# Attention and mixture of experts: the values of a pair of heads in three loads, with the global keys' rows copied on the chip

## The chip, the cores and the metric

One Trainium2 chip, one of its cores. The metric is device time of one execution in microseconds; the median of three runs of the kernel before is 718.49 us (716.6 to 720.79). A core has TensorE (PE, with its weight loads PEld), VectorE (DVE), ScalarE (ACT), GpSimd (POOL), SyncE (SP), which here issues the plain DMAs, and 16 DMA engines.

## The reference

Batch 8, 8 heads, 512 local and 32 global positions, head dimension 64. Per head, a global query attends to all 544 keys; a local query attends to the 32 global keys and to the local keys at most 32 positions away. Then each token of the 8 x 544 = 4352, with the 512 values of its heads side by side, goes to one of 8 experts (a greedy assignment with a capacity of 544 tokens each), and the expert applies two matrices with a ReLU between them.

```
s_g = scale * q_g @ k_all.T ;  out_g = softmax(s_g) @ v_all
s_l = scale * [q_l @ k_g.T , where(|i-j| <= 32, q_l @ k_l.T, -1e9)]
out_l = softmax(s_l) @ [v_g ; v_l]
x = heads side by side;  h = relu(x[mask_e] @ w1[e]);  out[mask_e] = h @ w2[e]
```

All data are float32.

## The kernel before

The attention comes first, then the routing (which token goes to which expert), then the experts. Only the attention's loads are changed.

**Keys and values by blocks.** Local positions are cut in 16 blocks of 32. A local block of queries needs its own block of keys, both neighbours, and the global keys: 4 x 32 = 128 rows, one matmul's width. On the host, `_blocks` puts a copy of the global block after every second local block, so that each such set of 128 rows lies together. For the values the 128 rows of a window lie along the partitions. The even windows are loaded: window w of head h is at `vw[:, 0, h, w]`, 65 columns (64 values and a column of ones, which sums the softmax). In an even window the partitions 0 to 31 hold the block before, 32 to 63 the global keys' rows, 64 to 95 the own block and 96 to 127 the next one. The rows of the global keys are thus the same in all 8 even windows of a head. The odd windows hold the same blocks at other partitions, and GpSimd makes them from the even ones with four copies (L119 to L122).

**Tiles.** A pair of heads (`b`, `p`; 32 pairs) has a tile `qk` (queries and keys, three loads) and a tile `vw` (128 partitions x 2 parities x 2 heads x 8 windows x 65). Seven buffers of each are in rotation. Before the change the even half is loaded in two DMAs, one per head, each 128 partitions x 2080 B; `load_v` is a generator that yields after each.

**Steps.** A step of the attention is a pair of heads with its local queries, or a batch entry's four pairs with their global queries: scores (`S`, on TensorE), mask and exp (DVE, ACT), transposes (`T`), evacuation by ACT, values (`O`: TensorE with weights `pt` and the tile vw, both parities), normalisation (DVE). The order of the steps' parts is written out by hand; all of TensorE's instructions of the attention come through one helper, so they have line L83 and are told apart by tiles.

**The order of loads.** A planner sorts the loads by the step that needs them. Each time that TensorE's issued work has grown by a fixed amount (by the kernel's own estimate) `tick` takes one piece: the next part of a generator. `paced` (L94) issues a DMA on SyncE's queue, which first waits for the last TensorE instruction issued before it. SyncE works through its queue in order. The first loads (L145 to L150) are issued without this order, before the steps begin.

**Stores.** The result of each batch entry goes to a buffer `xd` in DRAM, through the same queue. The experts later gather from it and from the weights with indirect DMAs that GpSimd issues; those run on a queue of their own.

Of the kernel before, what the change touches and what calls it, by code (L numbers as in the profile page):

```python
# [18 lines left out]
B, H, SL, SG, D = 8, 8, 512, 32, 64  # L19
# [44 lines left out]
def attention(ctx, tc, A, consts, xd, ident, L, nbatch, rt=None):  # L64
    nc = tc.nc
# [5 lines left out]
    qk, vw, xs, xg = {}, {}, {}, {}  # L71
# [21 lines left out]
    def paced(dst, src):  # L93
        d = nc.sync.dma_start(dst, src)  # L94
        if pe.last is not None:
            tc.add_manual_dep(d.ins, pe.last.ins.name,
                              mybir.DependencyInfo(mybir.DependencyClass.Sync, mybir.DependencyReason.DATA), reason="pace")
# [11 lines left out]
    def load_v(b, p):  # L109
        t = ld.tile([128, 2, 2, NW // 2, D + 1], F32, name="vw", bufs=7)  # L110
        vw[b, p] = t
        ev, od = t[:, 0], t[:, 1]
        n = NW // 2
        for h in range(2):
            w = n * (D + 1)
            paced(ev[:, h].rearrange("p w d -> p (w d)"), A["vw"][b, p, :, h * w:h * w + w])
            if h == 0:
                yield
        nc.gpsimd.tensor_copy(od[0:64], ev[64:128])  # L119
        nc.gpsimd.tensor_copy(od[64:96], ev[32:64])  # L120
        nc.gpsimd.tensor_copy(od[96:128, :, :n - 1], ev[64:96, :, 1:])
        nc.gpsimd.tensor_copy(od[96:128, :, n - 1:], ev[64:96, :, n - 1:])  # L122
        yield
# [22 lines left out]
    nc.sync.dma_start(mask.rearrange("p a b -> p (a b)"), A["mask"])  # L146
    nc.sync.dma_start(ident, A["ident"])
    now(load_qk(0, 1), load_v(0, 0))
    nc.sync.dma_start(wg.rearrange("p a b -> p (a b)"), A["wg"])
    now(load_qk(0, 2), load_v(0, 1))  # L150
    warm = ac.tile([128, 128], F32, name="warm")
    nc.vector.memset(warm, 0.0)
# [266 lines left out]
    for i, u in enumerate(steps):  # L419
        for q in [u[0].q] if isinstance(u[0], Local) else range(NP):  # L420
            for f, t in ((load_qk, i - LA), (load_v, i + 1)):
                k = f, u[0].b, q
                need[k] = min(t, need.get(k, t))
                left[k] = left.get(k, 0) + 1
# [784 lines left out]
```

## Time and profile before

| | before |
|---|---|
| median of the runs | 718.49 us |
| the profiled execution's own time | 718.45 us |
| its span, first to last instruction | 716.7 us |
| granted TensorE clock, mean | 0.968 |
| busy: PE, PEld, DVE, ACT, POOL | 657.4, 538.4, 477.0, 321.2, 223.0 us |
| read from and written to HBM | 83.49 and 17.83 MB |
| DMA queues, share of 16 engines over the span | q1 (SyncE's) 21.7%, q0 (GpSimd's) 20.4%, q8 (instructions) 0.7% |
| first to last load of values issued | 4.5 to 191.9 us |

A row of a group or a waits view names line, engine and operation, then what is written and read. In a view of waits the numbers are the microseconds in total, the times it happened and the longest. In a timeline they are the start, the duration over a merged row, and in brackets the idle time before it and what ended that; "issue" there is time in which the engine waited for nothing that the profile shows. The DMA share is the mean over the 16 engines.

### The profile page before, as it was taken

The page shows a single profiled execution, that of the slowest core. Times are in us where ns is not written, and L with a number is a line of the kernel's source. Part 1 is how long each engine was busy: PE and PEld are TensorE (multiplying, and loading weights), DVE is VectorE, ACT ScalarE, POOL GpSimd, SP SyncE. Part 2 cuts the span into 40 slices and gives each one's busy share as a digit, 9 for nine tenths or more (in the row PEclk, how much of TensorE's full clock was granted, in tenths as well). Part 3 has the DMA queues.
Part 4 walks back from the last instruction along what each step waited for, and adds up shares of the span by engine and source line. Part 5 has one row for each costly group of instructions (what it writes and reads, how often), then busy time and mean ns, then how long its engine had stood idle before and what let it go on. Part 6 is the DMA issues. An engine that isn't in the chain of part 4 may idle for free.

```text
span 716.7 us, 23878 instructions
## 1 busy us (share of the span) xinstructions
PE 657.4 (92%) x9972; PEld 538.4 (75%) x9972; DVE 477.0 (67%) x1758; ACT 321.2 (45%) x870; POOL 223.0 (31%) x249
## 2 busy tenths in 40 slices
PE   7797989889992599999999999999999999999997
PEld 6576666667771498778779879878978877988985
DVE  3678777787877887767767777767776774640510
ACT  5766767767840144343234244234333342641421
POOL 3565446654510500440240241142043025312002
PEclk9999999999995599999999999999999999999999
DMA  8788879887410530720540351162063065331001
GB/s 305 223 260 255 260 235 287 279 263 247 156 67 2 180 119 1 265 82 16 182 158 22 117 201 45 62 223 78 2 229 132 1 250 177 115 114 53 16 16 48
DMA packets 39580, 102.86 MB, mean 144 GB/s; under 512 B 4912, under 2 KB 14384, under 8 KB 35376
## 3 DMA queue, kind: packets, MB, share of 16 engines
q1 hardware_dynamic: 29232, 49.95, 21.7%
q0 software_dynamic: 10240, 51.39, 20.4%
q8 instruction: 78, 1.28, 0.7%
q14 instruction: 30, 0.25, 0.1%
HBM read 83.49 MB, written 17.83 MB: 141 GB/s over the span
## 4 chain that ended last, share of the span: by engine, by line
PE 76%; DVE 9%; issue 6%; DMA 4%; ACT 3%; POOL 1%; SPq 0%; POOLq 0%; DVEq 0%; ACTq 0%
PE H L1059 22%; PE Y L1087 21%; PE T L83 10%; PE S L83 7%; PE O L83 6%; PE R L617 4%; PE H L931 2%; DVE r_G L546 2%; DVE w2l L546 2%; PE Y L1077 2%; DMA xg<-xd,idx 1%; DMA out_dram<-y,idx 1%; PE Y L1107 1%; DVE r_pm L546 1%; ACT w2h L908 1%
## 5 line engine op out<-in xcount | busy, mean ns | idle before, releaser
L1059 PE MATMUL H<-xh,w1h 128*128 128x272 f32 x512 | 151.5, 296 | 1.9 <-DVE hl L546 1.5
L1059 PE MATMUL H<-xh,w1l 128*128 128x272 f32 x512 | 150.0, 293 | 0.0
L1059 PE MATMUL H<-xl,w1h 128*128 128x272 f32 x512 | 149.9, 293 | 0.0
L1061 ACT ACTIVATE hh<-H 128x272 fp32r<-128x272 f32 x128 | 50.9, 398 | 130.3 <-PE H L1059 125.8
L1087 PE MATMUL Y<-w2h,hh 128*128 128x512 f32 x256 | 103.9, 406 | 0.0
L1087 PE MATMUL Y<-w2l,hh 128*128 128x512 f32 x256 | 102.7, 401 | 0.0
L1087 PE MATMUL Y<-w2h,hl 128*128 128x512 f32 x256 | 102.4, 400 | 0.0
L1059 PEld LDWEIGHTS H<-xh,w1h 128*128 128x128 f32 x512 | 96.5, 188 | 5.3 <-DVE hl L546 2.5
L1059 PEld LDWEIGHTS H<-xl,w1h 128*128 128x128 f32 x512 | 96.5, 188 | 0.6
L1059 PEld LDWEIGHTS H<-xh,w1l 128*128 128x128 f32 x512 | 96.4, 188 | 0.3
L938 POOL DMA_INDIRECT out_dram<-y,idx x40 | 41.4, 1034 | 137.3 <-ACT y L1029 79.1
L173 ACT ACTIVATE p<-p,nm 128x128 f32<-128x128 f32 x256 | 78.0, 396 | 7.9 <-DVE nm L168 7.9
L168 DVE CUSTOM_DVE_ANT_0 p<-S,mask 128x128 f32<-128x128 f32 x256 | 56.7, 286 | 28.5 <-PE S L83 27.8
L546 DVE SCALAR_TENSOR_TENSOR hl<-H,hh 128x272 fp32r<-128x272 f32 x128 | 54.5, 434 | 23.6 <-ACT h L1063 12.8
L546 DVE TENSOR_TENSOR w2l<-w2r,w2h 128x512 fp32r<-128x512 f32 x64 | 43.2, 688 | 37.3 <-ACT w2h L908 36.9
L892 POOL DMA_INDIRECT w1r<-in_w_dram,widx x16 | 15.7, 980 | 163.0 <-DVE r_a L546 122.4
L83 PE MATMUL S<-qk 64*32 64x128 f32 (+2 forms) x2240 | 53.7, 299 | 12.2 <-issue 8.0
L1029 ACT ACTIVATE y<-Y 128x512 f32<-128x512 f32 (+1 forms) x40 | 23.2, 594 | 92.6 <-PE Y L1087 66.5
L119 POOL COPY vw<-vw 64x1040 f32<-64x1040 f32 x32 | 33.5, 1047 | 89.2 <-DMA vw<-in_vw_dram 51.3
L1087 PEld LDWEIGHTS Y<-w2h,hh 128*128 128x128 f32 x256 | 48.2, 188 | 15.7 <-issue 5.9
L908 ACT ACTIVATE w1h<-w1r 128x512 fp32r<-128x512 f32 x64 | 36.4, 622 | 47.1 <-DMA w1r<-in_w_dram,widx 47.1
L1087 PEld LDWEIGHTS Y<-w2h,hl 128*128 128x128 f32 x256 | 48.2, 188 | 10.0 <-issue 0.2
(177 smaller groups left out, 1214.0 us busy)
## 6 DMA issues: line engine op xcount, KB each, us to landing
vw<-in_vw_dram SPq DMA_DIRECT2D x64, 260.0 KB, 4.1
qk<-in_qk_dram SPq DMA_DIRECT2D x64, 216.0 KB, 3.7
qk<-in_qk_dram SPq DMA_DIRECT2D x32, 272.0 KB, 4.3
xd<-xs SPq DMA_DIRECT2D x28, 256.0 KB, 4.1
xd<-xs SPq DMA_DIRECT2D x1, 1024.0 KB
xg<-xd,idx POOLq DMA_INDIRECT x40, 3.6
out_dram<-y,idx POOLq DMA_INDIRECT x40, 2.8
cf<-in_cf_dram SPq DMA_DIRECT2D x1, 512.0 KB
```

Source lines behind the costliest of these rows:

```text
L83: s.last = op(o, w, x, **kw)
L119: nc.gpsimd.tensor_copy(od[0:64], ev[64:128])
L168: nc.vector.tensor_tensor_reduce(s.p[:, c, :], s.st[:, c, :], mask[:, c, :], -SCALE, BIG, ALU.add, ALU.min, s.nm[:, c:c + 1])
L173: nc.scalar.activation(s.p[:, c, :], s.p[:, c, :], AF.Exp, bias=s.nm[:, c:c + 1], scale=-1.0)
L546: return op(*args, **kw)
L617: s.nc.tensor.matmul(out, *args, **kw)
L908: nc.scalar.activation(hi, raw, AF.Copy)
L938: nc.gpsimd.indirect_dma_start(out=out, out_offset=bass.IndirectOffsetOnAxis(ap=rt.idx[ph][:n, t:t + 1], axis=0), in_=y[:n], in_offset=None)
L1029: nc.scalar.activation(y[:n], p[:n], AF.Copy)
L1059: nc.tensor.matmul(p, w[d][:, fs], x[:, d, q], start=(d + k == 0), stop=(d + k == 5))
L1061: nc.scalar.activation(hh[:, f, q], p, AF.Relu)
L1087: nc.tensor.matmul(p, h[:, f, q], w[f], start=(f + k == 0), stop=(f + k == 9))
```

## The change

The even half of a pair's values comes in three DMAs. The first brings, on partitions 32 to 63, window 0 of each head alone: 32 partitions x 2 heads x 260 B = 16,640 B. The second brings partitions 64 to 127 with all windows of both heads, 64 x 4160 B = 266,240 B. After the generator's yield the third brings partitions 0 to 31, 32 x 4160 B = 133,120 B. A new GpSimd copy, ahead of the four that there were, writes windows 1 to 7 of partitions 32 to 63 from window 0: 32 partitions x 2 x 7 x 65 elements. The four old copies, the arrays on the host and everything else stay as they were.

```diff
         n = NW // 2
-        for h in range(2):
-            w = n * (D + 1)
-            paced(ev[:, h].rearrange("p w d -> p (w d)"), A["vw"][b, p, :, h * w:h * w + w])
-            if h == 0:
-                yield
+        src = A["vw"][b, p].rearrange("p (h w d) -> p h w d", h=2, d=D + 1)
+        paced(ev[32:64, :, 0], src[32:64, :, 0])
+        paced(ev[64:128], src[64:128])
+        yield
+        paced(ev[0:32], src[0:32])
+        g = ev[32:64, :, 0:1]
+        nc.gpsimd.tensor_copy(ev[32:64, :, 1:], g.to_broadcast([32, 2, n - 1, D + 1]))
         nc.gpsimd.tensor_copy(od[0:64], ev[64:128])
```

## The prediction

> **What bounds the kernel now.** I read the page first: TensorE is busy nearly throughout, and there are three DMA queues that matter.
>
> ```profile
> PE 657.4 (92%) x9972; PEld 538.4 (75%) x9972; DVE 477.0 (67%) x1758; ACT 321.2 (45%) x870; POOL 223.0 (31%) x249
> q1 hardware_dynamic: 29232, 49.95, 21.7%
> q8 instruction: 78, 1.28, 0.7%
> ```
>
> Queue q1 carries all loads and stores of the attention. Queue q8 moves 1.28 MB in 78 packets, 16 KB each; TensorE has 2 x 9972 = 19,944 instructions, 256 to a packet, so I read q8 as the fetch of TensorE's program.
>
> The change touches only the attention, the first 213 us. The table of busy time by stage cuts it in the part with loads (35 to 185 us) and the tail, in which nearly all loads are done:
>
> ```profile
> 35.00:185.00 150.00, 132.99 (x4208) 101.92 (x4212) 116.22 (x654) 106.76 (x335) 81.94 (x101) 0.98 0.82 259
> 185.00:213.00 28.00, 27.28 (x837) 22.56 (x825) 21.68 (x114) 18.85 (x56) 8.40 (x11) 1.00 0.29 99
> ```
>
> The columns are stretch, length, then busy time of PE, PEld, DVE, ACT and POOL, the granted clock, DMA share and GB/s. With the DMA engines 82% busy TensorE idles 17.0 of 150 us; with them 29% busy it idles 0.7 of 28 us. The table of waits says for what, from 15 to 185 us and, last line, from 185 to 213 us:
>
> ```profile
> PE O L83 <- issue: 9.0, 9, 2.3
> PE S L83 <- issue: 8.0, 7, 2.2
> PE T L83 <- ACT p L173: 1.2, 1, 1.2
> PE S L83 <- DVE nm L168: 1.1, 1, 1.1
> PE T L83 <- issue: 1.0, 1, 1.0
> ...
> PE T L83 <- ACT xt L315: 0.7, 1, 0.7
> ```
>
> So 18.0 us in 17 waits are "issue": nothing in the program held TensorE back. No tile, DMA of data or engine costs it more than 1.2 us. One such wait, in the timeline, and the DMA queues in the stretch that ends with it (33.00 to 35.94 us):
>
> ```profile
> 35.94 0.42 PE L83 MATMUL O<-vw,pt 128*32 128x65 f32 x11 [2.34 <-issue]
> ...
> q1 hardware_dynamic: 502, 0.96, 89.3%
> q8 instruction: 1, 0.02, 2.1%
> ```
>
> TensorE stands still from 33.60 to 35.94 us, one fetch packet moves, and the engines are full of data. My reading: a fetch waits behind the data packets queued on its DMA engine, and TensorE runs dry. The attention is bound by TensorE plus the lateness of its program. A DMA therefore costs time here not by landing late but by standing ahead of a fetch.
>
> **The change, part by part.** First the load on q1 in that stretch (35 to 185 us):
>
> ```profile
> q1 hardware_dynamic: 22309, 38.16, 80.1%
> q8 instruction: 34, 0.56, 1.5%
> ...
> vw<-in_vw_dram SPq DMA_DIRECT2D x51, 260.0 KB, 4.1
> ```
>
> *Bytes.* 38.16 MB in 80.1% of 150 us is 318 GB/s while the engines work. A pair's values are two DMAs of 266,240 B: 532,480 B, 1.67 us of all 16 engines. These are 51 x 266,240 B = 13.6 MB of 38.16, 36% of the queue. After the change a pair has 16,640 B (32 partitions, two rows of 260 B each), 266,240 B on partitions 64 to 127 and 133,120 B on 0 to 31. The two large ones at 318 GB/s are 1.26 us. The small one is 64 packets: by bytes 0.05 us, and as 64 packets of the mean length (80.1% x 16 x 150 us / 22,309 = 86 ns) over 16 engines 0.34 us. I take 0.1, near the bytes, as its rows are a seventh of the mean packet. Sum 1.36 us, which is 0.31 us (19%) less, if the engines keep their rate.
>
> *Rate.* No load of before covers fewer than 128 partitions. The nearest rows are the scatters of the expert outputs, of 32 rows (window 310.80 to 311.40 us) and of 128 rows (318.75 to 319.75 us), each alone on the engines:
>
> ```profile
> DMA packets 32, 0.07 MB, mean 109 GB/s; under 512 B 16, under 2 KB 16, under 8 KB 32
> q0 software_dynamic: 32, 0.07, 46.1%
> ...
> DMA packets 80, 0.26 MB, mean 262 GB/s; under 512 B 16, under 2 KB 16, under 8 KB 80
> q0 software_dynamic: 80, 0.26, 68.9%
> ```
>
> Each has 16 packets of a few bytes that mark its end; the others are 4 KB. On 32 partitions one takes 46.1% x 16 x 0.60 us / 16 = 277 ns, on 128 it takes 68.9% x 16 x 1.00 us / 64 = 172 ns: 1.6 times as long on few partitions. These read SBUF and the loads write it, so the bounds for the loads are 1.0 (no such effect) and 2 (two engines take turns throughout; the 32-row case has one packet per engine, so they overlap in part only). I take 1.6, the one row there is: 1.26 x 1.6 + 0.1 = 2.11 us for a pair, 0.44 us (26%) more than now. With 2 it is 2.62 us, 0.95 us (56%) more.
>
> [...]
>
> *From the queue to TensorE.* How much stands ahead of a fetch? The view of the tile vw gives the time from issue to landing:
>
> ```profile
> L94 SPq DMA_DIRECT2D vw<-in_vw_dram x64: 327/332/1649, 4.5 to 191.9; - x64
> L119 POOL COPY vw<-vw x32: 1043/1046/1057, 10.2 to 195.8; 64x1040 f32<-64x1040 f32 x32
> L120 POOL COPY vw<-vw x32: 1042/1047/1057, 11.3 to 196.9; 32x1040 f32<-32x1040 f32 x32
> L121 POOL COPY vw<-vw x32: 940/941/949, 12.4 to 198.0; 32x910 f32<-32x910 f32 x32
> L122 POOL COPY vw<-vw x32: 291/292/293, 13.3 to 198.9; 32x130 f32<-32x130 f32 x32
> ...
> DMA to landing us min/median/max: 2.6/4.1/5.8
> ```
>
> The median is 1.5 us above the least, so I put the typical queue at 1.5 us; 36% of it is values. At 1.6 a fetch waits 1.5 x 0.36 x 0.26 = 0.14 us longer. There are 34 fetches in the stretch: 4.8 us if each of them passes it on, 2.4 us if only the 17 that are late now do. The other bound is that every added microsecond of the queue meets a fetch: 25.5 pairs x 0.44 = 11 us. I take 4.8, because a queue at 80% that gets 11 us (7% of the stretch) more work also makes fetches late that are in time today.
>
> *The start.* TensorE waits for queries and keys behind the first pair's values:
>
> ```profile
> 4.53 0.91 SPq L94 DMA_DIRECT2D vw<-in_vw_dram  x2
> 11.62 1.29 PE L83 MATMUL S<-qk 64*32 64x128 f32 x64 [1.42 <-DMA qk<-in_qk_dram]
> ```
>
> One pair is ahead of that transfer, so the wait moves by +0.4 us (bounds -0.3 and +0.9). The third issue, 0.46 us here, is hidden while the transfer is behind others on the engines; uncovered it would add that.
>
> *SyncE and GpSimd.* 32 more issues at 332 ns are 10.6 us for SyncE, which in the first 300 us spends more than that waiting for TensorE's pace:
>
> ```profile
> SPq L94 <- PE T L83: 62.2, 87, 5.1
> SPq L94 <- PE O L83: 47.0, 43, 9.5
> ```
>
> The new GpSimd copy writes 32 x 910 elements, as many as L121: 0.94 us a pair, 30 us in all. It waits for the small DMA; queued behind it are the pair's four other copies and, once, the clearing of pg (2.09 us from 17.95 us), which two more such copies move by 1.9 us to an end at 21.9 us, ahead of its first use at 24.19:
>
> ```profile
> 17.95 2.09 POOL L157 MEMSET pg<- 128x768 f32 x3
> 24.19 0.58 ACT L240 ACTIVATE pg<-S,gm 128x384 f32<-128x384 f32 x1
> ```
>
> In exchange the four old copies no longer need the last transfer (partitions 0 to 31 aren't among their sources), and the new one can run while partitions 64 to 127 are still on their way. The tightest place is the last pair:
>
> ```profile
> 191.25 0.95 SPq L94 DMA_DIRECT2D vw<-in_vw_dram  x2
> 195.81 1.05 POOL L119 COPY vw<-vw 64x1040 f32<-64x1040 f32 x1 [5.51 <-PE O L83]
> 198.85 1.60 PE L83 MATMUL O<-vw,pgt 128*32 128x64 f32 x95
> 198.88 0.29 POOL L122 COPY vw<-vw 32x130 f32<-32x130 f32 x1
> ```
>
> TensorE starts on these values as the last copy ends. Uncovered, the new copy costs 0.9 us there, once; started a DMA issue earlier it gains at most 0.3 us. I take 0. DVE and ACT get nothing new.
>
> *Sum.* The profiled execution took 718.45 us (span 716.7 and 1.75 around it; the median of the runs is 718.49, practically the same). 718.45 + 4.8 + 0.4 = 723.65 us. With the bounds of each term (2.4 to 11, and -0.3 to 0.9, last pair -0.3 to 0.9) this case spans 720.5 to 731.
>
> **The rivals.**
>
> *The bytes win.* If the loads to 64 and 32 partitions keep the full rate, the queue ahead of a fetch shrinks by 1.5 x 0.36 x 0.19 = 0.10 us, times 34 is 3.5 us, and 0.3 at the start: 714.65 us. For it: TensorE's idle falls with the DMA share in the stages. Against: the scatter rows. It decides if a packet on few partitions takes less than 1.25 times its usual time (1.25 x 1.26 + 0.1 = 1.67).
>
> *Nothing moves.* The "issue" waits could have a cost of their own, whatever the queue; then neither less nor more load changes them: 718.45 us. The tail without such waits speaks against it, but it also has other steps. [...] The same time results if bytes and rate just cancel.
>
> *Full contention.* If two engines take turns throughout (factor 2), a pair needs 0.95 us more; 25.5 of them are 24 us in 150, and the share goes from 0.82 to 0.98. The queue is then 1.5 x 0.36 x 0.56 = 0.30 us longer at least, times 34 is 10.3, and 0.9 at the start: 729.65 us. It decides where the engines have no idle time left.
>
> *GpSimd late.* If the copies depended on all three DMAs, each pair would be ready 0.9 us later; only the last pair has no margin: 719.35 us.
>
> **How the numbers follow.** Half a per cent, 3.6 us, is about what a measurement tells from no change. Chances: forecast 0.36 and full contention 0.12 (slower, 0.48 together); bytes win 0.24, of which 0.02 ends within 3.6 us (faster 0.22); nothing moves 0.25 and GpSimd late 0.03 (same 0.30). The forecast's own range is 720.5 to 731; to leave out no more than 0.2 it reaches down to 712, past the bytes' case, and to 731, past most of full contention.
>
> **What would show it.** In the stretch of loads: the mean length of q1's packets per byte (now 318 GB/s while busy; about 1.6 times slower on the values alone would bring it near 270), DMA share up from 0.82 in spite of 3.7 MB less, TensorE's "issue" waits up from 18.0 us by about 5, landing of the two large DMAs no earlier. If "issue" falls together with the DMA share, the bytes won; if it stays while the share moves, the fetch isn't the cause. The last pair's first GpSimd copy should begin before 195.8 us. A time above 731 or a wait for vw on TensorE in most steps would make the whole reading wrong.

## The result, and the profile after

| | before | after |
|---|---|---|
| median of 6 runs each | 719.04 us (716.6 to 720.79) | 725.33 us (723.07 to 726.75) |
| after / before, 95% interval | | 1.0094 [1.0067, 1.0122] |
| profiled execution, its span | 718.45, 716.7 us | 725.3, 723.5 us |
| mean granted clock | 0.968 | 0.970 |

The kernel is 0.94% slower. The prediction said 723.6 us with a range of 712 to 731, slower being the likeliest.

From the page of the kernel after, the busy times and the queue q1 that the prediction showed of before:

```profile
PE 657.5 (91%) x9972; PEld 538.2 (74%) x9972; DVE 478.4 (66%) x1758; ACT 320.9 (44%) x870; POOL 252.0 (35%) x281
...
q1 hardware_dynamic: 26672, 46.23, 21.5%
```

TensorE does the same work in the same busy time (657.4 us before, 657.5 after). GpSimd has 29 us more (the copies). Queue q1 moves 3.7 MB less than before, yet its share of the engines hardly falls (21.7% to 21.5%, of a longer span).

The table of busy time by stage, of after:

```profile
35.00:185.00 150.00, 127.64 (x4121) 97.57 (x4110) 113.17 (x629) 104.07 (x330) 104.05 (x123) 0.99 0.79 238
185.00:213.00 28.00, 27.50 (x860) 21.72 (x859) 22.31 (x124) 21.61 (x65) 13.32 (x17) 1.00 0.30 88
```

In the part with loads TensorE now idles 22.4 of 150 us instead of 17.0, with the engines *less* busy than before (0.79, was 0.82). In the tail it idles 0.5 us, before 0.7. The table of waits from 15 to 185 us, of after:

```profile
PE O L83 <- issue: 8.7, 14, 1.2
PE S L83 <- issue: 7.9, 6, 3.0
PE T L83 <- issue: 4.1, 3, 1.8
PE S L83 <- DVE nm L170: 2.2, 2, 1.1
PE S L83 <- DMA qk<-in_qk_dram: 1.7, 1, 1.7
```

"Issue" is 20.7 us in 23 waits, where it was 18.0 in 17, and a wait for queries and keys is new in this stretch. One profile each does not make much of the difference: in the first experiment below, where the time is that of before, "issue" is 15.4 us. The queue behind this, 35 to 185 us, of after:

```profile
q1 hardware_dynamic: 20218, 35.08, 77.6%
q8 instruction: 32, 0.52, 1.6%
...
qk<-in_qk_dram SPq DMA_DIRECT2D x49, 216.0 KB, 4.8
...
vw<-in_vw_dram SPq DMA_DIRECT2D x25, 260.0 KB, 4.2
...
vw<-in_vw_dram SPq DMA_DIRECT2D x25, 130.0 KB, 3.9
vw<-in_vw_dram SPq DMA_DIRECT2D x25, 16.2 KB, 4.2
```

35.08 MB in 77.6% of 150 us is 301 GB/s while the engines work; before it was 318. 25 pairs of values are 10.4 MB. If the other 24.68 MB still go at 318 GB/s (77.6 us), the values take 116.4 - 77.6 = 38.8 us, by this estimate 1.55 us a pair: less than the 1.67 of before, more than the 1.36 that were estimated for their bytes at 318 GB/s. Of the view of the tile vw, a row of before, and then rows of after:

```profile
L83 PE MATMUL O<-vw,pt x2048: 217/219/317, 14.8 to 208.3; 128*32 128x65 f32 x187
```

```profile
L83 PE MATMUL O<-vw,pt x2048: 217/219/317, 16.9 to 214.3; 128*32 128x65 f32 x187
...
L94 SPq DMA_DIRECT2D vw<-in_vw_dram x96: 326/588/1634, 4.5 to 198.6; - x96
...
DMA to landing us min/median/max: 2.4/3.8/5.5
```

In a row of this view stand the number of instructions, the least, median and greatest duration in ns, and the start of the first and of the last in us. TensorE's last matmul on a local step's values starts at 214.3 us instead of 208.3: 6.0 of the 6.8 us by which the span grew lie in the attention. The median issue of a load of values now holds SyncE for 588 ns, not 332. Attention ends of single profiles, which come from several chips, differ by some us (205.8 us in the profile of the first experiment), so the verdicts below rest on ratios and the profiles only show where to look.

### The profile page after: what moved, and what is told of

The parts are those of the page before. It is cut to its first block, busy times and chain, and to the rows that moved or that the text cites. A ratio compares the mean times of both kernels' runs of the same rounds, so it can differ in the third digit from the quotient of the medians.

```text
span 723.5 us, 23984 instructions
## 1 busy us (share of the span) xinstructions
PE 657.5 (91%) x9972; PEld 538.2 (74%) x9972; DVE 478.4 (66%) x1758; ACT 320.9 (44%) x870; POOL 252.0 (35%) x281
## 3 DMA queue, kind: packets, MB, share of 16 engines
q1 hardware_dynamic: 26672, 46.23, 21.5%
## 4 chain that ended last, share of the span: by engine, by line
PE 48%; DVE 3%; DMA 2%; issue 2%; ACT 1%; POOLq 0%; DVEq 0%; ACTq 0%
PE Y L1089 21%; PE H L1061 21%; PE R L619 3%; PE H L933 2%; PE Y L1079 2%; DVE w2l L548 1%; DMA w1r<-in_w_dram,widx 1%; DVE r_G L548 1%; ACT w2h L910 1%; DMA xg<-xd,idx 1%; PE Y L1095 0%; DMA out_dram<-y,idx 0%; DVE r_pm L548 0%; DVE w1l L548 0%; DVE hl L548 0%
## 5 line engine op out<-in xcount | busy, mean ns | idle before, releaser
L940 POOL DMA_INDIRECT out_dram<-y,idx x40 | 39.9, 997 | 135.8 <-ACT y L1031 82.2
L83 PEld LDWEIGHTS S<-qk 64*32 64x32 f32 x2240 | 33.2, 106 | 31.8 <-issue 19.5
```

Source lines behind the costliest of these rows:

```text
L83: s.last = op(o, w, x, **kw)
L940: nc.gpsimd.indirect_dma_start(out=out, out_offset=bass.IndirectOffsetOnAxis(ap=rt.idx[ph][:n, t:t + 1], axis=0), in_=y[:n], in_offset=None)
```

## The experiments

Each ratio is to the kernel before in runs on the same chip, with its 95% interval; the experiments ran on four chips, so two of them are compared by their ratios. A difference of two ratios has half-widths added in squares. The diffs show the lines that stand in place of the loads of before, or that are added to them; `src` is that of the change.

**1. The copy alone.** The kernel before plus the new copy after its loads.

```diff
+        g = ev[32:64, :, 0:1]
+        nc.gpsimd.tensor_copy(ev[32:64, :, 1:], g.to_broadcast([32, 2, n - 1, D + 1]))
         nc.gpsimd.tensor_copy(od[0:64], ev[64:128])
```

> The loads of before (two DMAs of 128 partitions, all bytes) with the new GpSimd copy added, which here writes again what the loads brought. Theory RATE (transfers to few partitions run slower, so the queue ahead of loads and fetches is no shorter): 719 us, no change. Theory ISSUE (the third DMA and its longer issue hold SyncE's queue, so that loads come later): 719 us. Theory COPY (GpSimd's added 0.94 us a pair makes the values late): 724 to 726 us, with waits of TensorE for GpSimd's copies.

Measured: 1.0011 [0.9978, 1.0045]. The copy costs nothing that can be told apart from none; it isn't the cause.

**2. Three DMAs, all bytes, all partitions.**

```diff
+        paced(ev[:, 0, 0], src[:, 0, 0])
+        paced(ev[:, 0, 1:], src[:, 0, 1:])
+        yield
+        paced(ev[:, 1], src[:, 1])
```

> All bytes of before, all on 128 partitions, but in three DMAs a pair (window 0 of head 0; windows 1 to 7 of head 0; head 1), no new copy. RATE: 719 to 720 us, since no transfer has few partitions. ISSUE: 722 to 726 us if an issue takes about 0.6 us as in the changed kernel, about 720.5 if it stays at 0.33 us. COPY: 719.

Measured: 1.0042 [1.0010, 1.0074], 3.0 us. The third issue has a price of its own, or the burst of two DMAs before the yield has.

**3. Both loads on half the partitions**, all bytes, no copy.

```diff
+        paced(ev[64:128], src[64:128])
+        yield
+        paced(ev[0:64], src[0:64])
```

> All bytes of before in two DMAs a pair, each on 64 partitions (64 to 127, then 0 to 63), no new copy. RATE: rows of 4160 B at 250 ns, eight per engine, are 2.0 us a pair where before takes 1.69, some 10 us more of queue time over 32 pairs: 723 to 727 us. ISSUE: two issues as before, 719 us, or 720 to 721 if an issue to few partitions is longer by itself. COPY: 719.

Measured: 1.0234 [1.0187, 1.0282], 16.9 us, the slowest of all and more than twice the expected 4 to 8 us, with the same bytes and the same number of DMAs as before. Queue q1 and then the tile vw, of this kernel:

```profile
q1 hardware_dynamic: 18428, 36.89, 85.9%
```

```profile
L83 PE MATMUL O<-vw,pt x2048: 217/219/317, 18.6 to 219.8; 128*32 128x65 f32 x187
...
L94 SPq DMA_DIRECT2D vw<-in_vw_dram x64: 465/477/1573, 4.5 to 203.5; - x64
...
DMA to landing us min/median/max: 3.3/5.1/8.1
```

The engines are busier for fewer bytes in the stretch (286 GB/s), the loads land 1 us later at the median, and each issue takes 145 ns longer than before.

**4. The change's bytes on all partitions.** Three DMAs of 16,896, 266,240 and 133,120 B, and a GpSimd copy in place of the bytes left out.

```diff
+        paced(ev[:, 1, 4, 0:33], src[:, 1, 4, 0:33])
+        paced(ev[:, 0], src[:, 0])
+        yield
+        paced(ev[:, 1, 0:4], src[:, 1, 0:4])
+        nc.gpsimd.tensor_copy(ev[:, 1, 4:], ev[:, 1, 0:4])
```

> The bytes and the number of DMAs of the changed kernel, but each on 128 partitions: 132 B rows, head 0 with 2080 B rows, windows 0 to 3 of head 1 with 1040 B rows. Windows 4 to 7 of head 1 are not loaded; GpSimd copies windows 0 to 3 there (about 0.3 us a pair), so the values of that head's last windows are not the reference's. RATE: a pair takes about 1.35 us of the engines where before takes 1.69, so the waits for the fetch shrink by 3 to 4 us: 714 to 717 us. ISSUE: three issues, as in the changed kernel: 721 to 725 us, 718 to 719 if issues stay at 0.33 us.

Measured: 0.9990 [0.9962, 1.0019], no gain where fewer bytes alone were expected to bring 2 to 5 us. Against experiment 2, with as many DMAs on as many partitions, the fewer bytes gain 0.52% (± 0.43). Against the change itself (1.0094), with the same bytes and number of DMAs, it is the partitions that cost: 1.04% (± 0.40), or the longer issues that come with them (median 588 ns against 382 here); experiments 8 and 9 separate these two.

**5. Loads with nothing beside them.** Eleven loads into an unread tile ahead of everything else, on various partitions.

```diff
+    sc = ac.tile([128, 1040], F32, name="sc")
+    sv = A["vw"][0, 0]
+    for lo, hi in ((0, 128), (64, 128), (0, 128), (32, 96), (0, 128), (0, 32), (0, 128), (0, 64), (0, 128)):
+        nc.sync.dma_start(sc[lo:hi], sv[lo:hi])
...
```

> The kernel before, with eleven loads of one pair's values put ahead of everything, each alone (it waits for the one before, which writes some of the same rows): 128 partitions between the others, 64 to 127, 32 to 95, 0 to 31, 0 to 63, and last the small one of 260 B rows and 128 partitions again. RATE, with partitions sharing ways in by halves (0 to 63 and 64 to 127): a 4160 B row takes about 165 ns on 128 partitions and on 32 to 95, which has both halves, and 250 to 320 ns on 64 to 127, 0 to 63 and 0 to 31. If few partitions are slow by their number alone, 32 to 95 is as slow as 64 to 127. If neither, all rows take about 165 ns and the slow rows of the changed kernel come from its company. ISSUE: the issues to few partitions take SyncE longer (about 0.6 us) than those to 128 (0.35 to 0.45 us) even with nothing else under way.

The DMA queues of this kernel while partitions 64 to 127 are loaded (4.38 to 7.95 us), then 0 to 127 (7.95 to 11.40), then 32 to 95 (11.40 to 14.27), and later 0 to 31 (17.75 to 20.09):

```profile
q1 hardware_dynamic: 80, 0.27, 28.8%
...
q1 hardware_dynamic: 144, 0.53, 49.2%
...
q1 hardware_dynamic: 80, 0.27, 32.5%
...
q1 hardware_dynamic: 48, 0.13, 19.8%
```

Share x 16 x length over the number of rows (64, 128, 64, 32; the 16 packets under 512 B that come with each load counted as nothing) is 257, 212, 233 and 232 ns for a row of 4160 B. By the same working partitions 0 to 63 take 238 ns, and the four other loads of 128 partitions from 198 to 214. So alone, few partitions cost here 1.1 to 1.25 times per row, much less than the scatter rows' 1.6 and less than expected. These are single loads, and equal ones differ by 8%: that 32 to 95 would be faster than 0 to 63 or 0 to 31, as expected of halves, is not shown here.

**6. One load for all**, 128 partitions x 4160 B.

```diff
+        paced(ev.rearrange("p h w d -> p (h w d)"), A["vw"][b, p])
+        yield
```

> All bytes of before on 128 partitions in one DMA a pair (rows of 4160 B), no new copy. ISSUE: one issue less a pair than before takes off about what the third one added in the kernel with three full DMAs (0.4%): 0.995 to 0.998 of before. RATE: rows on 128 partitions keep their rate, 1.00; if rows of 4160 B were the cause and not the partitions, it is slower, 1.01 or more. A burst twice as long ahead of a fetch could cost some of the gain: up to 1.005.

Measured: 1.0036 [1.0006, 1.0066]. One issue fewer gains nothing when its 532 KB come at once. Whether the burst takes the gain away, or that a pair's loads are now one piece of the pace less, is not shown. Rows of 4160 B are not slow in themselves here: queue q1 in 35 to 185 us has 321 GB/s, before 318.

```profile
q1 hardware_dynamic: 18282, 37.47, 77.7%
```

**7. A slower pace of the loads**, on the kernel before.

```diff
-        if pe.work >= 0.62:
-            pe.work = min(pe.work - 0.62, 1.0) if piece() else 0.62
+        if pe.work >= 0.66:
+            pe.work = min(pe.work - 0.66, 1.0) if piece() else 0.66
```

> The kernel before with each load issued after 0.66 instead of 0.62 us of TensorE's work by the kernel's own estimate, in all three places of that constant. If the queue ahead of the fetch sets TensorE's idle time, loads spread out further leave it shorter: 0.993 to 0.998 of before, with fewer waits for issue than 18 us between 15 and 185 us. If the queue doesn't matter: 1.00. If loads then come too late: above 1.003, with waits for DMA of qk or vw.

Measured: 1.0044 [1.0008, 1.0080], not the gain that was expected of a shorter queue. The "issue" waits are 12.2 us where before has 18.0, a wait of 2.2 us for queries and keys came up, and the kernel was no faster. The waits from 15 to 185 us, of this kernel:

```profile
PE O L83 <- issue: 6.0, 8, 1.5
PE S L83 <- issue: 5.4, 5, 1.9
PE S L83 <- DMA qk<-in_qk_dram: 2.2, 1, 2.2
...
PE T L83 <- issue: 0.8, 1, 0.8
```

**8. The change without its small DMA.** GpSimd fills partitions 32 to 63 from elsewhere.

```diff
+        paced(ev[64:128], src[64:128])
+        yield
+        paced(ev[0:32], src[0:32])
+        g = ev[64:96, :, 0:1]
+        nc.gpsimd.tensor_copy(ev[32:64], g.to_broadcast([32, 2, n, D + 1]))
```

> The changed kernel without its small DMA: the global keys' rows are not loaded, and GpSimd's new copy fills all eight windows of partitions 32 to 63 from window 0 of partitions 64 to 95 (1.05 us a pair), so the values of the global keys are not the reference's. The two large DMAs stay. ISSUE: two issues instead of three, about 0.4% less than the changed kernel: 1.004 to 1.006 of before. RATE alone: the large DMAs decide, 1.008 to 1.010.

**9. The same on the middle partitions.** Two loads of the same bytes on 64 and 32 partitions, but the first on 32 to 95.

```diff
+        paced(ev[32:96], src[32:96])
+        yield
+        paced(ev[0:32], src[0:32])
+        nc.gpsimd.tensor_copy(ev[96:128], ev[64:96])
```

> As the kernel without the small DMA (two DMAs of 64 and 32 partitions, one added GpSimd copy of 1.05 us), but the large DMA brings partitions 32 to 95 instead of 64 to 127, and GpSimd fills 96 to 127 from 64 to 95, so the values of those rows are not the reference's. Same bytes, same number of DMAs and of partitions in each. RATE by halves of the partitions: the large transfer now reaches both halves, its 4160 B rows take about 200 ns as in the kernel with one load, the mean over all values' rows falls from 250 to about 220 ns, and the time is 1.000 to 1.004 of before. If the number of partitions decides, or ISSUE: 1.006 to 1.010, as without the small DMA (1.008).

Measured: 1.0079 [1.0047, 1.0111] for 8 and 1.0012 [0.9985, 1.0039] for 9. The two kernels differ in nothing but which partitions the first load and the copy take, and their ratios by 0.67% (± 0.42). Against the change itself, experiment 8 has the third DMA less and gains 0.15% (± 0.42): here the third issue has no price that can be told from none. Queue q1 from 35 to 185 us, first of 8, then of 9:

```profile
q1 hardware_dynamic: 18323, 35.01, 77.7%
```

```profile
q1 hardware_dynamic: 17944, 34.30, 72.5%
```

300 GB/s against 315. By the working used above (399,360 B a pair, 25 pairs, the rest at 318 GB/s) a pair takes by estimate 1.51 and 1.29 us; its bytes at 318 GB/s are 1.26. On 32 to 95 the penalty is nearly gone, though the issues are no shorter (medians 476 and 522 ns). The traces have each packet's time, so this can be seen without the subtraction: from 35 to 185 us a packet of 4160 B, which only loads of values have, takes on average 210 ns in experiment 6 (128 partitions), 217 in 9, 245 in the change, 247 in 8 and 263 in 3. That partitions share their ways in by halves, as the expectation has it, was the author's assumption: the direction agrees (217 against 247 ns), the cause is not shown.

**10. Half of the bytes.** Only the first head's values are loaded; the second gets a copy of them.

```diff
+        paced(ev[:, 0].rearrange("p w d -> p (w d)"), A["vw"][b, p, :, :w])
+        yield
+        nc.gpsimd.tensor_copy(ev[:, 1], ev[:, 0])
```

> The kernel before with only head 0's values loaded (one DMA of 128 partitions, 2080 B rows); GpSimd copies them to head 1 (about 0.55 us a pair), so head 1's values are not the reference's. 8.5 MB and 32 DMAs less. RATE, that is, the queue ahead of the fetch sets TensorE's idle time: the queue loses about 27 of 155 us, and of 18 us of waits for issue some 6 to 10 go: 0.985 to 0.992 of before. If the bytes on the queue don't matter to TensorE: 1.00. ISSUE alone: 32 issues less, 0.996.

Measured: 0.9948 [0.9913, 0.9982], less than expected of the queue; the 0.996 expected of the 32 issues alone lies in the interval. The queue and, in the second fence, the waits from 15 to 185 us, of this kernel:

```profile
q1 hardware_dynamic: 18650, 31.43, 66.3%
```

```profile
PE O L83 <- issue: 6.5, 9, 1.8
PE S L83 <- issue: 5.8, 9, 1.4
...
PE T L83 <- issue: 0.3, 1, 0.3
```

The waits are 12.6 us, about as few as in experiment 7, where the queue is hardly shorter (78.9%). And 80.1% - 66.3% of 150 us is 20.7 us of queue, for 3.8 us of time (0.52% of 723.07): some 0.2 us per us of queue, and part of that may be the issues'.

**11. An almost empty DMA more for each pair** (64 B), on the kernel before.

```diff
+    tiny = ac.tile([16, 8 * 32], F32, name="tiny")
...
+        k = 4 * b + p
+        paced(tiny[:, 8 * k:8 * k + 1], A["vw"][b, p, :16, :1])
```

> The kernel before with one DMA more a pair that moves almost nothing (16 partitions x 4 B into a tile that nobody reads), issued ahead of the first of the pair. ISSUE: 1.003 to 1.005 of before, if a third issue of 0.35 to 0.6 us on SyncE is what the kernel with three full DMAs pays. If the third issue is hidden by SyncE's waits for TensorE's pace, as the prediction had it: 0.999 to 1.001.

**12. Two of them, but none in the first four pairs**, whose loads stand at the start: 56 DMAs.

```diff
+        for i in range(2 if b else 0):
+            paced(tiny[:, 8 * k + 4 * i:8 * k + 4 * i + 1], A["vw"][b, p, :16, :1])
```

> The kernel before with two of the almost empty DMAs a pair (16 partitions x 4 B into a tile that nobody reads), but only from the second batch entry on: 56 added issues in the paced part and none before or in the first steps, where the kernel with one a pair for all pairs had four. If ISSUE costs in the paced part, where SyncE waits for TensorE's pace: 1.005 to 1.008 of before, with the end of the attention later by 3 to 6 us. If its cost lies at the start, where SyncE issues without a break and TensorE waits for the first queries and keys: 0.999 to 1.002.

Measured: 1.0034 [1.0006, 1.0062] for 11 and 1.0071 [1.0046, 1.0096] for 12: 2.4 us for 32 added issues and 5.1 us for 56, 0.08 and 0.09 us each. So added DMAs cost in the paced part too, not only at the start, and SyncE's waits do not hide them. Of experiment 12, in three views: queue q1 in 35 to 185 us, TensorE's waits for "issue" from 15 to 185 us, and SyncE's waits over the first 300 us:

```profile
q1 hardware_dynamic: 23666, 37.91, 78.3%
```

```profile
PE O L83 <- issue: 12.3, 9, 2.5
PE S L83 <- issue: 7.3, 8, 1.8
PE T L83 <- issue: 3.0, 3, 1.4
```

```profile
SPq L94 <- PE T L83: 46.5, 67, 5.1
SPq L94 <- PE O L83: 36.3, 30, 8.9
...
SPq L94 <- DMA qk<-in_qk_dram: 10.0, 18, 2.5
```

The engines are no busier than before, yet "issue" went from 18.0 to 22.6 us. SyncE waits less for TensorE's pace (82.8 us in these two rows, 109.2 before) and now 10.0 us for landings of qk (0.4 before, 1.7 in experiment 11). The trace's semaphores tell what these waits are: this program's plain DMAs use eight semaphores in turn (100 and 102 to 108, for all 201 DMAs of before and all 233 of after), and each wait is for the DMA issued eight places earlier, which has to land first. Two added DMAs in a row bring that limit nearer, so part of experiment 12's price may be this wait and not the issue; experiment 11 and the change (2.0 us) hardly meet it.

## Why the prediction was right, and which steps failed

**The sum.** Forecast +5.2 us; measured 6.85 us between the profiled executions, and 0.94% of 719.04 us, 6.8 us. The experiments split it so:

| part | forecast | measured |
|---|---|---|
| GpSimd's copy | 0 | +0.1% ± 0.3 (1) |
| SyncE's third issue | 0 | +0.34% ± 0.28 (11) to +0.42% ± 0.32 (2): 2.4 to 3.0 us; +0.15% ± 0.42 (after against 8) |
| fewer bytes | -0.31 us of queue a pair | -0.52% (4 against 2): -3.7 us |
| half the partitions | +0.75 us of queue a pair | +0.67% (8 against 9) to +1.04% (after against 4): 4.8 to 7.5 us |
| start | +0.4 us | not measured alone |
| last pair | 0 | 0 |

With 0.34, 0.67 and the other parts the sum is 0.1 + 0.34 - 0.52 + 0.67 = 0.6%, with the larger figures 1.04%; 0.94% lies between. This is no sharp test: each part is uncertain by 0.3 to 0.4%, and the larger figure for the partitions uses the change's own time. Bytes and partitions together come to +1.1 to +3.8 us, where the forecast had 4.8; the third issue, which it left out, adds up to 2.4 to 3.0 us. (The bounds of the forecast's terms add up to 720.25 and 731.25, not 720.5 and 731.)

**Loads to few partitions run slower per byte: right, mis-sized.** The factor was taken as 1.6 from the scatter rows; it is about 1.2 (245 to 263 against 210 ns a packet, 1.51 against 1.26 us a pair). So "DMA share up from 0.82" failed: it fell to 0.79, and the rate is 301 GB/s, not 270. The 0.1 us for the small DMA holds: alone it takes 4.6% of 16 engines over 2.03 us, 0.09 us of all 16, and in the trace of after its packets of 260 B take 22.7 ns on average (35 to 185 us), 64 x 22.7 / 16 = 0.09 us.

**From the queue to TensorE: the conversion failed.** By it, a pair of 1.55 instead of 1.67 us shortens the queue by 7%, 1.5 x 0.36 x 0.07 x 34 = 1.3 us faster. The time rose. How much time a microsecond of queue costs is not one number here:

- By bytes, experiment 10: 20.7 us of queue less (and an issue a pair less) gained 3.8 us (1.3 to 6.3), some 0.2 us per us. Experiments 2 and 4, with as many issues (1.70 and 1.40 us a pair, 3.7 us gained), give 0.5, but within 0.1 to 0.9.
- By partitions, experiment 9 against 8: (1.51 - 1.29) x 25 = 5.5 us of queue less, 4.8 us (1.8 to 7.8) gained, 0.9 us per us.
- By partitions, experiment 3: the engines are busy 85.9% instead of 80.1% and move 3% fewer bytes in it, some 13 us more for the same bytes. It cost 16.9 us (13.5 to 20.3), 1.3 us per us.

Only the first and the last are clearly apart. That time on slow partitions costs more than time on bytes is one reading; another is that a microsecond of queue costs more the busier the engines already are (66 to 80% in experiment 10, 80 to 86% in 3), and no run separates the two. Two errors met in the forecast: a factor too large, and a conversion too small for it. That the sum came out near is luck in the sizes, and by the forecast's own working so is the sign: with the factor at 1.2 a pair takes 1.61 us, less than the 1.67 of before, and it would not have said slower. That loads on half the partitions cost time is shown by experiments 4, 8 and 9; in 8, as in the change, they do so while the engines are less busy than before.

**Issue waits up by about 5: not shown.** They are up 2.7 us, of TensorE's 5.4 us more idle time in the stretch, while the DMA share fell, a case that the prediction's signs do not have; 1.7 us is a wait for queries and keys. One such "issue" wait in the timeline of after, with the queues in the stretch that ends with it (94.2 to 97.2 us):

```profile
97.20 1.09 PE L83 MATMUL S<-qk 64*32 64x128 f32 x27 [3.01 <-issue]
```

```profile
q1 hardware_dynamic: 466, 0.85, 83.5%
q8 instruction: 1, 0.02, 1.9%
```

It has the form of the one shown before: one packet of queue q8, and engines that q1 keeps 83.5% busy. That these waits are waits for a fetch is the prediction's reading of q8 (19,944 / 78 = 256 instructions a packet). The packets' times in the traces agree with it: all 17 of before end 1.2 to 1.5 us after a packet of queue q8 has ended, and 22 of the 23 of after 1.2 to 1.6 us, though such packets come only 3.3 to 6.3 us apart. That a fetch stands behind data packets is not shown, nor that the waits' sum follows the load on the engines: it is 12.6 us with half of the values' bytes (queue q1 at 66.3%), but 12.2 in experiment 7 (78.9%) and 18.3 in 9 (72.5%). Nor do they carry the price of half the partitions: they are 18.2 us in the profile of experiment 8 and 18.3 in that of 9.

**SyncE hides 32 more issues in its waits for pace: wrong.** This term of the sum was put at nothing. SyncE did wait 109 us for TensorE, yet an added DMA with hardly a byte in it costs some 0.08 us of the kernel's time (11; 0.01 to 0.14), and a third DMA of all partitions 3.0 us in all (2). A possible reason is that each issue stands behind one such wait and ahead of the next; that is argued, not shown. In the change itself the price was neither found nor excluded (0.15% ± 0.42 against experiment 8). The prediction also priced all issues at 332 ns; the three of the change have a median of 588. Of after, the first issues:

```profile
4.51 1.98 SPq L94 DMA_DIRECT2D vw<-in_vw_dram  x3
```

Three issues take 1.98 us, where two took 0.91. What the start costs is open: the first matmul on values comes at 16.9 us instead of 14.8, but at 15.6 and 16.4 us in the profiles of experiments 1 and 7, whose first loads are those of before. That the longer issues cost time themselves was not shown: those of 9 are as long as those of 8, and 9 isn't slower than before.

**The last pair, 0: right.** SyncE's issue and GpSimd's copies in the timeline of after:

```profile
197.23 2.29 SPq L94 DMA_DIRECT2D vw<-in_vw_dram  x3
...
200.49 0.94 POOL L120 COPY vw<-vw 32x910 f32<-32x910 f32 x1 [5.19 <-DMA vw<-in_vw_dram]
...
204.67 0.29 POOL L124 COPY vw<-vw 32x130 f32<-32x130 f32 x1
```

The pair comes 6 us later as a whole, so the clock time given for its first copy (before 195.8 us) failed, but that copy starts 3.3 us after the issue, where it was 4.6, and from issue to the end of the last copy it takes 7.7 us; it took 7.9.

**The rivals.** "The bytes win" needed less than 1.25 times the usual time per packet. The queue did meet that condition (245 against 210 ns, 1.2), and the kernel still lost: the condition, not only the chance, was wrong. "Nothing moves" fell with the result, 1.0094 with an interval above 1. Full contention fell (share 0.79, not 0.98); that two engines take turns, its factor of 2, was the author's assumption, and the factor measured is about 1.2. "GpSimd late" fell with experiment 1.

**Open.** Which way the load on half the partitions delays TensorE beyond its time on the queue, and how an almost empty DMA does. Some of these runs have later landings (3), some more "issue" waits (3, 12), but no run here changes one of these alone, and the single profiles of before and of experiment 1, of equal time, differ by 2.6 us in "issue".

## What to carry to other kernels

A load that left out bytes was not cheaper here when it also left out partitions: 22% fewer bytes of values on half of the partitions cost 0.94%, on all of them, with as many DMAs, they cost and gained nothing. Where a part of the partitions must do, try 32 to 95 and not 64 to 127, which was 0.67% faster here for the same bytes, and count every DMA that is added to a queue paced by another engine, even an almost empty one, which cost some 0.08 us here. And before a queue's length is turned into time, measure that conversion: it was 0.2 us per us in one experiment on this queue and 1.3 in another.

## What the runs showed of the hardware that was not expected

- How long SyncE took to issue a DMA differed with its shape, 0.34 to 0.64 us, though not with that alone (64 to 127 takes 0.59 us here, and issues of values have a median of 476 ns in experiment 8). In the timeline of experiment 5 stand, each behind an idle queue, partitions 64 to 127, 0 to 127, 32 to 95, 0 to 31, 0 to 63 (rows of 4160 B), the small DMA (32 partitions x 2 rows of 260 B) and 0 to 127 again; the second number is the duration in us:

```profile
4.38 0.59 SPq L148 DMA_DIRECT2D sc<-in_vw_dram  x1
7.95 0.34 SPq L148 DMA_DIRECT2D sc<-in_vw_dram  x1
11.40 0.58 SPq L148 DMA_DIRECT2D sc<-in_vw_dram  x1
...
17.75 0.34 SPq L148 DMA_DIRECT2D sc<-in_vw_dram  x1
...
23.55 0.49 SPq L148 DMA_DIRECT2D sc<-in_vw_dram  x1
...
30.35 0.64 SPq L149 DMA_DIRECT2D sc<-in_vw_dram  x1
32.38 0.34 SPq L150 DMA_DIRECT2D sc<-in_vw_dram  x1
```

- Which partitions a load wrote changed its packets' time while other transfers ran: 247 ns for 4160 B with 64 to 127 and 0 to 31 (experiment 8), 217 with 32 to 95 and 0 to 31 (experiment 9), with 0.67% of the whole kernel behind it. Alone the difference is no clearer than that between equal loads (experiment 5: 257 ns on 64 to 127, 233 on 32 to 95, and 198 to 214 in five equal loads of 128 partitions).
- TensorE's "issue" waits were waits for its program, if queue q8 is its fetch: in the profiles of before and after 39 of the 40 between 15 and 185 us end 1.2 to 1.6 us after a packet of queue q8 has ended.
- A DMA of 64 B cost this kernel some 0.08 us (experiment 11); leaving out one of 266,240 B, its issue included, gained 3.8 / 32 = 0.12 us (experiment 10). So much of a load's cost may lie in the issue; experiment 6, with an issue fewer but all bytes in one burst, didn't gain it.
